# Another order of issue for a fused attention and feed-forward kernel, and its last 26 unread products left out

## The chip, the cores and the metric

The kernel runs on one core of a Trainium2 chip. The metric is the device time of one execution in microseconds, 303.65 us as the median of three runs of the kernel before. One more execution was recorded by the hardware profiler; its trace is what the views below are taken from. The engines are TensorE (PE in the views, its weight loads PEld), VectorE (DVE), ScalarE (ACT), GpSimd (POOL) and SyncE (SP), which issues nearly all DMAs. Each works through its own instructions in the order in which the program gives them, and waits on semaphores for the others.

## What is computed

Attention in which each query sees only the keys that share its nearest centroid, then a feed-forward block with SiLU:

```
q, k, v: (4, 8, 768, 64)   centroids: (8, 16, 64)   w_in: (512, 2048)   w_out: (2048, 512)
q_assign = argmax(q_n . c_n);  k_assign = argmax(k_n . c_n)
mask = q_assign[:, :, :, None] == k_assign[:, :, None, :]
scores = where(mask, (q k^T) / sqrt(64), -1e9);  attn = softmax(scores);  x = attn v
h = x @ w_in;  out = (h * sigmoid(h)) @ w_out          # x as (3072, 512), out (3072, 512) float32
```

## The kernel before

`build` (line 174) makes a graph of 1,913 steps: it says what each step does, on which engines it may run, after which steps, and with which buffers. It gives no order. The order stands in `PLAN` (line 20), a compressed list of numbers worked out beforehand by a search over a model of the engines. The list has two parts: for each of 1,307 uses of a buffer, which of the pool's buffers it gets (`POOLS`, line 138: for instance 8 banks `M` of PSUM, 20 tiles `P`, 4 tiles `hl`); then pairs of a step's number and the choice among its engines. The kernel function (line 823) unpacks the list and issues the steps one after the other (line 861). A negative number stands for products of zeros on TensorE that nothing reads. So the list alone decides which engine does what, in which order each engine works, and which buffers have to come free. The costs in the graph (`act_w`, `dve_w`, `pool_w`, lines 158 to 169) belong to the search; the kernel does not use them when it runs. In them a VectorE instruction costs 62 ns and about 1.04 ns for each element, whatever went before it.

The steps that the text speaks of, with their lines:

- Loads (L224, L243, L274, L279): k and q rows (`nat`), v rows (`nv`), the weights in 16 pieces through `gq`. All but one are issued by SyncE.
- Preparing a head (`part`, line 373). `hi` rounds the rows to float16 (L413 on ScalarE, L415 on VectorE, L417 on GpSimd) and `lo` makes the remainder (L421, VectorE). Both are turned around: by products with an identity on TensorE (L447), settled by a copy (L463 ScalarE, L465 VectorE), or by a DMA transpose that SyncE issues (L474) and that waits for `lo`. Then come the products with the centroids (L488, L493), sums and peaks (L502, L540, L545), a one-hot mark (L507, L549), its turn (L447 or VectorE's L562), and the writing of the marks under the turned rows: L525 and L527 in the one form, four writes a part on GpSimd (L574), ScalarE (L576) or VectorE (L578) in the other.
- `attention` (line 593): score products (L619), the exponential on ScalarE (L625), products with v (L642), the reciprocal and the scaling on VectorE (L658, L661), a turn to the layout of the next stage (L679 by DMA; L689 on TensorE with L696 on VectorE).
- `mlp` (line 705): products with w_in (L721), tanh on ScalarE (L727), the gate on VectorE (L730), products with w_out (L747), a copy out of PSUM (L760 ScalarE, L762 VectorE) and the store (L765). Casts of the weights stand at L293 (GpSimd) and L297 (VectorE), those of v at L254 (GpSimd) and L256 (ScalarE).

Batch 0 has its queries in two rounds (columns 0 to 1, then 2 to 5), so that feed-forward products are to be had early; the other three batches have one round. The list weaves attention of one batch with the feed-forward of the batch before, so that TensorE has something to do while ScalarE takes the exponentials. Some products of zeros (L865) stand at the start, where TensorE has nothing else. Behind the list, lines 873 to 879 issue 26 more products of zeros (L877) into four banks; nothing reads them.

Of the kernel before, what the change touches and what calls it, by code (L numbers as in the profile page):

```python
# [17 lines left out]


PLAN = (  # L20
    "c-mFk1-uqT8^+;%`*hOX-5^MZ(%mH`CEbl8DT+u*qY{F2gMxs9AWA6UM+r)!f=Y;hQs4ico%5>lyLcuxW~X+~LC0|%kK=XR|2+KhnOwl}lMXr|"
# [4 lines left out]
    "%egV8ML{zIlFe8LO`jy#bR_i=X3m5-H)QS@YwzujPQ2+^kEx5ceU@lO-fe?p#@EA@f+ihf`_MgC;}kS~;jT_SZ?w6mJD=S)d(BuTnszv*-*mkQ"
    "^Tht}z7Vvdl`?*QJHy?)-;R^l^qJcS{(r4OPk2p+%&{Ib6CE=Tg5jeQ%-FkYGSbY#fVqdyjHRD8rCd4M%(bBD<v6=zBvY=nl4PF7ZB4+e-hgdi"
    "l1XVr`Ak2k=i+Vae5Oxz)hOG_l=&G)j3vgHdk4&HP=6%ad;3hw0%q>Vo9hSdeiCC=zdOH^%{mL2D<zoc^PAPDzKgVTRlSmEuI@GWNwT|Og6T{3"
    "ZL-;2^!$FiXL`&%-TQlKPtcA}gzfP_cz^STcR!Drd%l0|`aZj^+%@e!lh=-K%3kV(S7E?j#~Y3w`zO)vPeD8L6HG6J%%2FjD@*^ym|k*MdaT`j"
    "eYWrPgvsIddh9zSXlAI-j&sQDQ2}$^lzHcv8SnOGw7G_R#VFG=p74IF^Wx1tJ*F<&)M(uY?QY<;JB81@1AJyA<IKAxV0ZbD8IwpeXEd9F;ob<@"  # L30
    "nV(>v*KbSRwUdk}GY{PNiRNOQnN3=Cj(Hl#zVW>Ft>_Jx`NONseUtj_%JPTDz#Cq7{&25&Z5x6n25hf-?Hk<ppYiqD9nLY)Z})>>c;)-;xcI`e"
    "%WL2H?w;n@`QWzGXUqNex;{I{LiYK5;WEeG(P!@NGpoaE`_vO|XTa_?e%tnxz6jap_u7&3hi7Xb+)npv=AStpwC4o=^<Ci)-_H~Ny72wy9>MT;"
    "lGpATA=~qQD`<DTkbQ1{_zdSi*LR=E^PkoQ>@Jit^Mm2@QpU?;cPYm{z1Qwj-f%zr?QZXu1Z*$6JGsxU0k3`HpuMKgj$O#MEojFuWXIDNeh-K2"
    "4(tm*jpJkw&jfdtK6{qR9JdgQ%vyKMuBvrboil0>pFRsYwd_8nFO8bEmlDi-*>PT>tPZg@@$oaiQ<roP^h7VTLwj^UJ=8}7G(tzaYd1t=(!Gg&"
    "&=;wZ2A%LNj^QZ!AqT!eTJ*<2<TSg#<1|52G(&T|hxhR^I-@JPV*vO2nfMDn!Uwp4oA?#K;V_P13szz)(jfyDqYJv3=MFfRNMFDe^Zs(2C0L3N"
    "sZUQ_#sIV+UdHdZiWSr?$1-H6J|}XcC3UUr+wmf9;Wl2yYiNU)I41|kW<+c9d5CQ(%j9wQu3Y#GtB{$pEXaja<hS7(uHz?Ur92yo;yIMY=ad&G"
    "-XWgCU7XhQP_~-525YenZ(uSCQn#MCiFRzn8PX*v`ycTvPNF3FF~q{eyeNe2<d35m>5qwfaRT|s=f@|cOA)^(p2H68#CdGS1{9&bJ{q7Q8etIS"
    "gHeF=>%_6xjh5tFp*h|pUxxTRYT^K@qby#)IO@N{1Pnn7%4%T`>2kyw#7R8siy8~k`-wA&vrw6I6;wnejHhfO$5tiX80Ap`P4Fpo`|t(c!W8V%"
    "e5Y<du?F#N;vnJ(3`0}3m$EO_HjN9`pc<xXZ4lof4%K=fJruQ32h%ifDgOb(Fp{#u#4MOj-EiV?%2r|(>SC~c`GnxnxL^k&GzZl#s(-{N4ys3f"
    "B<azl*OGpsd8;|9@%Hd8C&nNWQFxd7*_flXNq!*y)LPY=AU@C@Li)b;4dPeYdo*9LQ*%l4T<bz}hByxkxc5`-bC`?y<j+z+3ZwBgWq;tF))x8K"  # L40
    "&<^d<N$Wv-2C<;lH1Q!Zlh!@yL;Bt$_Q1=Un>eU7LOg?W@WKZ_vQn3d_!seS?T@6pq8qMbHXdm`X$>J3aR_KVBZv)%M=$i&+{IYUL8L|>9M)Rq"
    "Iva_7k%%;S14T5ih;Jc}`h%Dj6Oj&cut{?s3y>ZeH1D)#wT3jeHCM3<yRj7u^&Grdwh$+2o?`;?(MQ*abFm!T)b|{>S$$31L;OsANP04Hk)Dfm"
    "Pkhb<>qVTUu_C^TshZE2r}?5ejOpl3T>;GpVjuKHXLLbV6z7Fk0wqxj?`iBcuB6{5et^X&L;g98;hfh|m~;{Br7iu)=Oukedj)YHaS4{<2#%sZ"
    "#|%Je>WgX5AUzS2P)P47;vfu0K90$c5Y~`ii!xgOtc~+r>j&+P)cr`jfQz`QeVOC-VjtFF1!Y5sLop0Rb#H7^KWj{|9vkp0*M5i_JkL$e`%UwQ"
    "@^KiCN}N{@%hjL66~s#%bD4AMlmCePU*xZF{z}r7DO*L{if!14?f6@BS^Et2b+KDxjasB@V>Rh2#OJk-ll~OnaQwG=|4>$1-zU^Zqbfe8{u6wL"
    "7s*%0?;Lwf^N_OR8VBMDy=!RON%aZG48<wZ%c%Ph-)UX3C~Ht&6J_xM<%_WdA89`$_M^N%(sS$p;y}$Ey@T{l)H@B2Id(qBeyM$&d|AB@IIcW~"
    "VK^!vBW`ibZM~aFH$*kOfHrs)ui*~$ckzezJ<Q_T6)A74Ympv-_M|&tB<V)P7HEma=!Wj-h)!sNrf7x-^vOMR=R<H1`N3#~7{nnSeb5D6(Hed6"
    "HTOA$!+42&J3OInPqpWf?u;*}+mC1Nho^HDN5~(=0o<p23T1EOOY$D|3x|#%9wa}K_?6Z+u8^LtxqulsNSkMB4N+cB`?>l=-(Te4Ast|RrYen0"
    "n5OgLquft?1wHT<$G(ecT8reT5Z~7P)psoU03XR;aWAjtJbGfK<~9<Mgk+?`o4Ou)p*OzeI&Tms<7fPWwOEHy7>ye^rsK4pw5O53to6qJn1-9C"
    "!(`1r$}?-u)2=GirKbE%wO#W?-|@6FJuj4>v>#LUI>urg?(@v!i8t{p7HOZuQY^z2^(k>C9^x;}3#7#-*nz*XkmK@jpDd)aVm9VzpVV5>+@&3>"  # L50
    "iP?}H$2mSX$M@hR_o4O<?TuKhYtz=*TC+UMcJe1k=g@wqv0*MoQ=frzmypj%`xjCF9xuH8<PYFG(m(6{L3$qMBe&)pc3~^FX@9^1wH?199oL*d"
    "%!ND}BlSNbDZk1+PHO+qy2NcnQ68bSN<2mUAII$0v*Dc9ChpO`6U6fxW35%jW<BXW*nmg4#(AfSXK<4ADO@9c7>~7f@Ko!L`#jS;<@w9`yiOtV"
    "g>hE<2Qe1cwcn9%jvD0uP=9D`={eM9Y}7uF&1y6Lq)j{RkB<eo_EFN`;564dgYQWXp{^Ht<5Tj3h=Y*{nel_(ImkjfE1pL-<luU9xW-()Ysi1D"
    "_aX|CE&?wukiUpa@Q@#eNq7xo@CM3a00!b5*UCj4kM~JeAjTmcIk{f~F%d~fP5vF?Gz`OVe5pM|`-k=_OrUHc-o{k?q&-o6srg3igT6S=z1|{D"
    "(Y!@J^hAF>KXo;U*}2~a;vuaw;#ef3D7H|RhWcWpi=zZCQx+taL|r^b{YGMGVm;y}Y{m$T)L84AhxjI@V+K-T0jje$J|yNMmLZnHa`g%Mg~T5@"
    "_X6gSo{JUu2zfCN6;TP>upO0A1xqmsqt)N|09Ek<ZLEf6r03%z*Y3u>UL`#fv+yo<U?*PW*ppf-Xsdqa_@D87kmp8el)+-HZ9Jy#2^NulPji{{"
    "Jv`NWMQg$RXBuZ6>H27ZU-Yh^thLrA8lnx_p%LZlHOJX=wh*^!{!!+GANgo|eqsR>#JAKR!(aL~(f0=F8)`4dl|^HYX@U^tE3r!BM)@w{O^$nn"
    "vef^oy^Qh}q^oPpbshYvZyRDATtOL*nS^q}vA3zegS)89i|K34E3~Ap6>6%@<X2;j?x}qW$8iGJv<^5XNzcPIYY~6rTIGqq6Z2EHR^x_Cx-R)!"
    "l-H)d5&6bwqIsh=ibB-aW(=E>j^>ycL?9AT=t})Oy|0MvHSa0=S!06xls`bM#)kTbx<BO=$d|y!q(4C`>H_40>Q~fetU6HM5xcPmowVMmi$_WH"
    "rf<q~UPaQmiJxho!FSk;efUCakoscyAL#^Q8;)&@%%m%!GD@KenxcZPiBzOhV>oST#<^)o*Py(Pkgkh9qz`Cs(HbIM8TBZCftZDu74=Bh$4J`y"  # L60
    "E5{ww_k-3Fb=7pN#z*6Th1~0?_E5@3an4KV$$9OFz0|)Lf$Y@hz&Bdw#9WxqxwWW!nX(SV=DaHolRkoGx)=3b8OP?DN5sAylbiH;>hlm!YpjW9"
    "wBMjJ=U*pw(ffvD(^B`n(!}B@g1l%!SvQW2<(Oprq;XRJp$LlNvGz*chjd<~<Gg-EFMN2Su~yq@<7na(o;f427&4(a5|M<G)TQVA45-TSQ^}{M"
    "{CCX};v!_EE<N!@;yKFGlFooCD8cb*h?BKvVF5nJ-yHV{-!n&VX;0?bw~4d0*J}*9)@#HucpU@KMe~&Mjz~woI&lv%9yLghB~C;G(hczr>Akq4"
    "wvvBa^A-b93i~xjbvzpC`x}k)?SmNYJ?=jbI9)k+JooNQdJFDxo`>kyI>H2uLpP3lkN7_FY2PB=)m~0)#`!I@4s>7qsr9ON4CPtK52K$J6PI8J"
    "mf`{R2Q*GxYb)^^e2ZnAbA)&lS@9LV)_T`Is&@<NAeLi0o@yV*P}1GG)+^|NY2>Hl4?PpsVLh^GK68)k#1JCzNbfz$W)NqhkiLnDD=-TmYu+Ie"
# [757 lines left out]
def kernel(  # L823
# [49 lines left out]
    free = sorted(last, key=last.get)[:4]
    for rows, count in ((128, 3), (64, 6), (128, 2), (32, 8), (64, 2), (32, 4), (128, 1)):
        for i in range(count):
            r0 = i * rows % 128
            e.nc.tensor.matmul(  # L877
                e.T["M"][free[i % 4]][:, 0:256], e.zeros[r0 : r0 + rows, 0:128], e.zeros[r0 : r0 + rows, :], start=True, stop=True
            )


# [28 lines left out]
```

## Time and profile before

| | |
|---|---|
| median of three runs (lowest, highest) | 303.65 us (303.47, 304.11) |
| the profiled execution's own time | 304.88 us |
| its span, first to last instruction | 303.1 us |
| mean granted TensorE clock in it | 1.000 |
| DMA read and written | 27.30 MB and 6.29 MB |

The profiled execution took 304.88 us, of which 303.1 us are the span that the views show and 1.78 us lie around it; it was 1.23 us above the median. Busy times of TensorE include a modelled end of each product, so idle time that the views give for it is a lower bound.

### The profile page before, as it was taken

The numbers are of one execution on the slowest core, as the hardware profiler recorded it, in microseconds if no ns is written. First come the engines' busy times: TensorE is split into PE (matmuls) and PEld (weight loads), VectorE is DVE, ScalarE is ACT, GpSimd is POOL, SyncE is SP. The second block draws the span as 40 slices with busy tenths as digits, with TensorE's granted clock in tenths as the row PEclk, the third lists the DMA queues.
The fourth block names the chain that finished last, engine by engine and source line by source line (L and its number), as shares of the span: only waits on it lengthen the run. The fifth ranks groups of instructions, "written<-read, shape, count | busy, mean of one in ns | idle before, by whom it ended". The sixth has DMA issues, their size and how long they took to land.

```text
span 303.1 us, 7937 instructions
## 1 busy us (share of the span) xinstructions
PE 295.3 (97%) x3080; PEld 184.4 (61%) x3080; DVE 210.9 (70%) x519; ACT 232.1 (77%) x478; POOL 76.2 (25%) x144
## 2 busy tenths in 40 slices
PE   8888999999999999999999999999999999999998
PEld 5656776646565566666665656566666555565445
DVE  4899999999897697789999997446742312377310
ACT  3799999989989798999967888899896650468101
POOL 2534556263630436243303333000000000000000
DMA  6999999999699999998978955111000521400022
GB/s 200 313 236 163 199 263 288 251 287 247 194 241 234 274 206 263 253 297 194 266 208 149 239 89 115 26 71 28 0 3 0 64 61 28 160 15 0 35 97 79
DMA packets 80182, 48.00 MB, mean 158 GB/s; under 512 B 57360, under 2 KB 75152, under 8 KB 80144
## 3 DMA queue, kind: packets, MB, share of 16 engines
q1 hardware_dynamic: 79856, 47.39, 66.9%
q8 instruction: 24, 0.39, 0.6%
q10 hardware_dynamic: 288, 0.10, 0.1%
q14 instruction: 14, 0.11, 0.1%
HBM read 27.30 MB, written 6.29 MB: 111 GB/s over the span
## 4 chain that ended last, share of the span: by engine, by line
PE 79%; DVE 9%; DMA 6%; issue 2%; ACT 1%; SPq 1%; POOL 1%; POOLq 0%; DVEq 0%; ACTq 0%
PE M L747 27%; PE M L721 24%; PE M L619 16%; PE M L642 9%; DMA nv<-in_v_dram 2%; DVE hl L421 2%; PE M L493 2%; DMA gq<-in_moe_w_in_dram 2%; DMA nat<-in_k_dram 2%; DVE ab L578 1%; DVE gq L730 1%; ACT P L625 1%; DVE ab L527 1%; DVE M L540 1%; PE M L877 1%
## 5 line engine op out<-in xcount | busy, mean ns | idle before, releaser
L625 ACT ACTIVATE P<-M 128x512 f16<-128x512 f32 x288 | 154.8, 621 | 17.0 <-PE M L619 16.2
L721 PE MATMUL M<-xt,win_s 128*128 128x384 f16 (+2 forms) x512 | 94.3, 325 | 0.6 <-DVE gq L730 0.4
L747 PE MATMUL M<-wout_s,gq 128*128 128x512 f16 (+1 forms) x400 | 91.4, 370 | 0.0
L730 DVE SCALAR_TENSOR_TENSOR gq<-tn,M 128x384 f16<-128x384 f32 (+2 forms) x128 | 65.9, 548 | 35.0 <-ACT tn L727 34.0
L619 PE MATMUL M<-ab 80*128 80x256 f16 (+1 forms) x384 | 87.7, 326 | 2.1 <-DVE ab L527 1.0
L727 ACT ACTIVATE tn<-M 128x384 f32<-128x384 f32 (+2 forms) x128 | 60.6, 513 | 15.8 <-PE M L721 12.1
L721 PEld LDWEIGHTS <-win_s 128*128 128x128 f16 x512 | 49.1, 97 | 34.6 <-issue 0.7
L747 PEld LDWEIGHTS <-gq 128*128 128x128 f16 x400 | 38.5, 97 | 37.8
L642 PEld LDWEIGHTS <-P 128*128 128x128 f16 x1152 | 42.5, 97 | 8.4 <-issue 1.2
L619 PEld LDWEIGHTS <-ab 80*128 80x128 f16 x384 | 33.3, 97 | 20.4 <-DVE ab L527 1.9
L642 PE MATMUL M<-vt,P 128*128 128x65 f16 x1152 | 45.1, 193 | 0.4 <-DVE oh L549 0.4
L574 POOL TENSOR_SCALAR ab<-ohT 16x384 f16<-16x384 f16 (+1 forms) x54 | 29.2, 544 | 62.1 <-PE M L619 19.6
L421 DVE SCALAR_TENSOR_TENSOR hl<-nat,hl 128x384 f16<-128x384 f32 (+1 forms) x60 | 36.6, 626 | 0.6 <-ACT hl L413 0.4
L760 ACT COPY ot<-M 128x512 f32<-128x512 f32 (+1 forms) x16 | 9.0, 560 | 26.8 <-PE M L747 21.1
L417 POOL TENSOR_SCALAR hl<-nat 128x384 f16<-128x384 f32 (+1 forms) x35 | 19.2, 559 | 22.9 <-DMA nat<-in_k_dram 8.5
L540 DVE TENSOR_REDUCE M<-M 128x192 f32<-128x384 f32 (+1 forms) x28 | 15.1, 541 | 6.9 <-PE M L493 6.6
L661 DVE TENSOR_TENSOR xn<-M,rz 128x384 f16<-128x384 f32 (+2 forms) x40 | 18.7, 472 | 0.9
L762 DVE COPY ot<-M 128x512 f32<-128x512 f32 x9 | 6.0, 683 | 18.7 <-PE M L747 18.7
L254 POOL CAST vt<-nv 128x384 f16<-128x384 f32 x25 | 14.4, 589 | 15.4 <-DMA nv<-in_v_dram 14.9
L562 DVE STREAM_TRANSPOSE ohT<-oh 128x384 f16<-128x384 f16 (+1 forms) x28 | 15.5, 555 | 0.8
L578 DVE TENSOR_SCALAR ab<-ohT 16x384 f16<-16x384 f16 (+1 forms) x43 | 14.6, 342 | 1.2
L493 PEld LDWEIGHTS <-ab 128*128 128x128 f16 x320 | 11.7, 96 | 6.2 <-issue 1.5
(51 smaller groups left out, 145.3 us busy)
## 6 DMA issues: line engine op xcount, KB each, us to landing
nv<-in_v_dram SPq DMA_DIRECT2D x16, 384.0 KB, 5.2
out_dram<-ot SPq DMA_DIRECT2D x23, 256.0 KB, 2.5
nat<-in_k_dram SPq DMA_DIRECT2D x15, 384.0 KB, 5.2
nat<-in_q_dram SPq DMA_DIRECT2D x12, 384.0 KB, 4.6
gq<-in_moe_w_in_dram SPq DMA_DIRECT2D x8, 512.0 KB, 6.4
gq<-in_moe_w_out_dram SPq DMA_DIRECT2D x8, 512.0 KB, 5.6
nat<-in_q_dram SPq DMA_DIRECT2D x4, 256.0 KB, 5.5
ab<-hl SPq DMA_TRANSPOSE x32, 4.7
```

The lines of the kernel that those rows point to most:

```text
L417: e.nc.gpsimd.tensor_scalar(out=dh, in0=src, scalar1=sign[kind], scalar2=1.0, op0=ALU.mult, op1=ALU.mult)
L421: e.nc.vector.scalar_tensor_tensor(out=dl, in0=src, scalar=sign[kind], in1=dh, op0=ALU.mult, op1=ALU.subtract)
L540: e.nc.vector.tensor_reduce(out=sums(), in_=bank(Lb)[:, 0 : 32 * n].rearrange("p (n c s) -> p n c s", s=2, c=HC), axis=AX.X, op=ALU.add)
L574: e.nc.gpsimd.tensor_scalar(out=dst, in0=src, scalar1=OHV, scalar2=1.0, op0=ALU.mult, op1=ALU.mult)
L619: e.nc.tensor.matmul(bank(sb)[:, at : at + 128 * (c - a)], ab[0:80, kt[m], :], ab[0:80, qt[a] : qt[a] + c - a, :].rearrange("p n c -> p (n ...
L625: e.nc.scalar.activation(out=T(P)[:, 0:n], in_=bank(sb)[:, 0:n], func=AF.Exp, bias=0.0, scale=-ESC if negated(b, h) else ESC)
L642: e.nc.tensor.matmul(bank(O)[:, (D + 1) * t : (D + 1) * t + D + 1], T(P)[:, at : at + 128], T(vb)[:, VW * m : VW * m + D + 1], start=(m == ...
L661: e.nc.vector.tensor_tensor(out=T(xn)[:, 0:nq, (h % 2) * D : (h % 2) * D + D], in0=o3()[:, :, 0:D], in1=T(rz)[:, 0:nq].unsqueeze(2).to_bro ...
L721: e.nc.tensor.matmul(bank(bk)[:, 0:n], e.win_s[:, r, ts(fb, 128)], T(X)[:, r, 128 * j0 : 128 * j1], start=(r == 0), stop=(r == NR - 1),)
L727: e.nc.scalar.activation(out=T(tn)[:, 0:n], in_=bank(bk)[:, 0:n], func=AF.Tanh, bias=0.0, scale=1.0)
L730: e.nc.vector.scalar_tensor_tensor(out=gq(fb // 4)[:, fb % 4, 0:n], in0=T(tn)[:, 0:n], scalar=1.0, in1=bank(bk)[:, 0:n], op0=ALU.add, op1= ...
L747: e.nc.tensor.matmul(bank(bk)[:, 0 : c1 - c0], gq(quarter)[:, fc % 4, ts(t, 128)], e.wout_s[:, fc, c0:c1], start=(fc == 0), stop=(fc == NF ...
```

## The change

Two things are changed: the text of `PLAN`, and the products behind the list.

```diff
 PLAN = (
-    "c-mFk1-uqT8^+;%`*hOX-5^MZ(%mH`CEbl8DT+u*qY{F2gMxs9AWA6UM+r)!f=Y;hQs4ico%5>lyLcuxW~X+~LC0|%kK=XR|2+KhnOwl}lMXr|"
...
+    "c-l>x2i#B9AII;#zxC{C?-dedWMyRUjBMF^@7+KW*|Q?0tO$h?)juQ3C=w!4A(cuplPLf9=iKxBJTI^J^ZB0dIrrRi&-tG3xxf43IF92wo)fTt"
...
 )
@@ -857,7 +858,6 @@
-    last = {}
     for at in range(0, len(order), 2):
@@ -866,17 +866,6 @@
             s.fn(list(s.engines)[choice])
-            for b in s.use:
-                if b.pool == "M":
-                    last[b.i] = at
-
-    free = sorted(last, key=last.get)[:4]
-    for rows, count in ((128, 3), (64, 6), (128, 2), (32, 8), (64, 2), (32, 4), (128, 1)):
-        for i in range(count):
-            r0 = i * rows % 128
-            e.nc.tensor.matmul(
-                e.T["M"][free[i % 4]][:, 0:256], e.zeros[r0 : r0 + rows, 0:128], e.zeros[r0 : r0 + rows, :], start=True, stop=True
-            )
```

The graph, the costs in `build` and the pools stay as they are. The model with which the new list was searched took VectorE to need extra time between two steps of different kinds; that model is not part of the kernel. Unpacked, the two lists hold the same 1,913 steps. 1,048 of the 1,307 buffer numbers differ, and these steps change their engine:

| steps | before | after |
|---|---|---|
| writes of the marks, VectorE / ScalarE / GpSimd | 56 / 18 / 54 | 44 / 18 / 66 |
| `hi`, VectorE / ScalarE / GpSimd | 10 / 15 / 35 | 12 / 8 / 40 |
| casts of the weights, VectorE / ScalarE / GpSimd | 4 / 0 / 12 | 1 / 1 / 14 |
| casts of v, ScalarE / GpSimd | 7 / 25 | 5 / 27 |
| copies after a turn (L463, L465), VectorE / ScalarE | 2 / 3 | 1 / 4 |
| copies of the output, VectorE / ScalarE | 9 / 16 | 17 / 8 |
| products of zeros at the start, in their groups | 20, 7, 4, 5 | 20, 7, 4, 1, 4 |

Everything else keeps its engine, but not its place. Two marks serve to compare the orders, since TensorE has done the same work at them in both lists. Mark A is the first score product of batch 1: 143 steps of TensorE stand ahead of it in both lists, the same ones but for four. Mark B is the first score product of head 2 of batch 1, with 192 steps ahead of it in both. An engine's list up to the last of its steps that TensorE's steps ahead of the mark depend on has this many steps:

| | VectorE | ScalarE | GpSimd |
|---|---|---|---|
| up to mark A, before / after | 118 / 107 | 79 / 78 | 38 / 47 |
| up to mark B, before / after | 154 / 136 | 110 / 107 | 53 / 64 |

By kind, VectorE's list up to mark A has seven writes of marks of 16x256 (L578) fewer, and one each fewer of: cast of a weight (L297), copy of 128x1024 after a turn (L465), `hi` of 128x384 (L415), sum (L540), peak (L545), copy of 128x512 (L696); and one more write of marks of 16x256 in the other form (L527) and one more `hi`, of 128x512 (L415). ScalarE's up to mark A has one exponential (L625), one `hi` of 128x512 (L413) and one write of 16x256 (L525) fewer, one copy of 128x1024 after a turn (L463) and one write of 16x256 (L576) more. GpSimd's has eight writes (L574) and a cast of a weight more. VectorE's up to mark B has seven writes (L578), the weight's cast (L297), the copy (L465), three `hi` of 128x384 (L415), three `lo` of 128x384 (L421), three gates of 128x512 and two of 128x256 (L730) fewer, and the same two more.

ScalarE's list begins with `hi`, two small copies of the centroids, `hi`, a copy of 128x512 (L463) and one of 128x1024, a write (L525) and two exponentials before; after, with `hi`, the two small copies, a copy of 128x512, one of 128x1024, two writes (L525), two more copies of 128x1024, and then the exponentials. SyncE's list has the same loads and transposes; the first five loads are the same, then loads of v and of q change places, and the pieces of w_in come in the order 1, 4, 5, 0, 2, 3 in place of 4, 0, 1, 2, 5, 3, with the same transposes between them. The last four products with w_out, the copy of their 128x256 by ScalarE and its store end both lists.

More of the change, by code (lines that the diff above doesn't have):

```diff
@@ L26 @@
[L26 to L65, printed above, removed]
@@ new lines @@
+    "9aDCkkP}41PQ>_vlvVFgQaNmJO$+~e*Z4!m>zN*0u9Y1$cGz4Qq3oG<zIwK`$|2iF#1O;|T90Gz?U?(!=3mBGJ=3de?ie&ZyXG!_-$5r0PbyYC"
+    ">X>@9Q|}>jSI68f5z-lBis?BFsd!?d<5RnMG?gpU?Oj7ok|_n8IPmYLKGV=-@XYwtCWanksYyV?X1p1*6g1a(=2?@?ll#5-&#fN9kYwA(;7c&0"
+    "Q(eT&sK?knGw-pGX4k~U8)C!}(<;H<KVVi%bC7KB9X6hb=^@3`g|QON>getfM&odQ*UXM<yqe!sGv5J56fsw%L}$st7i*r}$rMW&^XQrpJNEhf"
+    "bqv|Io^9=#xy@K_C%W3MohvWub))wTa!-$^3fpLK%)0BjGzST0T_Uz^x}CqE8F$dkK&puWf2BOzyZQ)oZP45$-b7c}tVh7MOgGnhcK)?W$=E5B"
+    "v=)if#o5S?n5%;}hC-$X^{bWfd(t(I8G~z{)H6N0riT>Mf6%V3Yf2e=C_TFKTyytCdk5VqEjmN4d9H}LYn-tn=6*3IDix)kjRijj{MZWF>%B}X"
@@ L76 @@
+    "_eb;<oi}>#(|0*oO1ZP%5wJVy9SB<M+YLOb-@96Co!{6sv@Y0hz(t*Rl<VnRmwt~jmfUC?=mK4#0W{P%EA1=Ve-CA`yXkwTawNP7%eb~2zV7-B"
+    "teAx}a2Ee^bOo%0Rg_n24kC;nDnJ=13*{gJF%S!X)9x1hqxGV^23-qp>Aj79)}!YjJ9RnWs@}EWy59XLSAnV!go;oJDnkgu5C`#)0L`E|w16h?"
+    "7&L|3I-|5FwceCFLMO-xxga;xfSPcFHh<||UF$@-CDejeP!H-u1Nf8r%i6o}pYnnK-=3V>PzUNlLudqz!37TjPz|cXqmTlrkOu9bJ#>K1&;=49"
+    "36dcX<b{0D8rnb~=nMUzEp&zcFd)LYj%I<Za7pimXi+Ez#bF=}g8QKa<c9(<7=}PWC<KLJC=`JQpd^%n2jL+o4a2x!H?%wSfZ@;+dg1Slj)0Lc"
+    "3P!^i7z_Ug)Mn7m"
 )
```

59 lines of the change are left out of this document (45 added, 14 removed).

## The prediction

> **What bounds the kernel now.** I read the page's busy line first, then the table of busy time by stretch, then TensorE's waits in the early part.
>
> ```profile
> span 303.1 us, 7937 instructions
> PE 295.3 (97%) x3080; PEld 184.4 (61%) x3080; DVE 210.9 (70%) x519; ACT 232.1 (77%) x478; POOL 76.2 (25%) x144
> ```
>
> TensorE is busy for 97% of the span. A new order can win only where TensorE idles, so the question is where that is. The table by stretch has, after the stretch and its length, the busy time of TensorE, its weight loads, VectorE, ScalarE and GpSimd with their instructions, then granted clock, DMA share and GB/s:
>
> ```profile
> core 0: us, PE busy (x) PEld busy (x) DVE busy (x) ACT busy (x) POOL busy (x), PEclk, DMA share, GB/s
> 7.15:25.00 17.85, 15.29 (x238) 11.46 (x239) 15.87 (x42) 14.86 (x28) 7.05 (x11) 1.00 1.16 258
> 25.00:50.00 25.00, 24.06 (x424) 18.05 (x420) 23.54 (x76) 24.30 (x50) 15.00 (x27) 1.00 1.07 239
> 50.00:76.00 26.00, 24.72 (x246) 15.59 (x246) 25.00 (x57) 24.27 (x54) 12.06 (x19) 1.00 1.09 253
> 76.00:120.00 44.00, 43.48 (x476) 26.29 (x475) 34.76 (x84) 39.02 (x81) 17.86 (x31) 1.00 1.02 236
> 120.00:251.40 131.40, 131.40 (x1380) 81.94 (x1379) 89.40 (x215) 109.04 (x227) 21.99 (x40) 1.00 0.54 121
> 251.40:299.90 48.50, 48.50 (x277) 26.64 (x274) 19.38 (x39) 17.72 (x39) 0.00 (x0) 1.00 0.18 62
> ```
>
> From 120 us to the last useful product TensorE has no idle time that this view shows, and VectorE and ScalarE have plenty. Before that it idles for 17.85 - 15.29 = 2.56 us, then 0.94, 1.28 and 0.52 us: 5.30 us in all, a lower bound, since the ends of products are modelled. From 25 to 76 us VectorE is busy for 48.54 of 51 us and ScalarE for 48.57: two full queues feed an engine that is nearly full itself. What TensorE waits for from 7 to 76 us (total, times, longest), the first three rows:
>
> ```profile
> engine line waited for: us in total, times, longest us
> PE M L619 <- DVE ab L527: 1.0, 2, 0.8
> PE M L493 <- DVE gq L730: 0.7, 1, 0.7
> PE M L447 <- DVE hl L421: 0.5, 2, 0.3
> ```
>
> VectorE is the one that ends these waits. So the early part is a race of VectorE's and ScalarE's lists against TensorE's, and after 120 us the work of TensorE alone counts, which the change does not touch.
>
> **The change part by part.** First mark A, the first score product of batch 1. TensorE does the same work ahead of it in both lists, and the trace has it here, in the timeline:
>
> ```profile
> 52.91 0.60 PE L619 MATMUL M<-ab 80*128 80x256 f16 x3
> ```
>
> VectorE's list up to there loses and gains the kinds that the section on the change names. Their rows from the groups by shape, the last figure before the idle time being the mean of one in ns; the last three serve for mark B:
>
> ```profile
> L578 DVE TENSOR_SCALAR ab<-ohT 16x256 f16<-16x256 f16 x7 | 1.8, 259 | 0.2
> L297 DVE CAST win_s<-gq 128x1024 f16<-128x1024 f32 x1 | 0.8, 820 | 0.0
> L465 DVE COPY ab<-M 128x1024 f16<-128x1024 f16 x1 | 0.7, 690 | 0.2 <-PE M L447 0.2
> L415 DVE TENSOR_SCALAR hl<-nat 128x384 f16<-128x384 f32 x10 | 4.7, 475 | 0.1
> L540 DVE TENSOR_REDUCE M<-M 128x192 f32<-128x384 f32 x24 | 13.5, 560 | 6.9 <-PE M L493 6.6
> L545 DVE TENSOR_REDUCE mx<-M 128x12 f32<-128x192 f32 x24 | 8.5, 353 | 0.6
> L696 DVE COPY xt<-M 128x512 f16<-128x512 f16 x4 | 1.7, 419 | 0.0
> L527 DVE TENSOR_SCALAR ab<-M 16x256 f16<-16x256 f16 x6 | 1.7, 289 | 0.2
> L421 DVE SCALAR_TENSOR_TENSOR hl<-nat,hl 128x384 f16<-128x384 f32 x48 | 27.9, 596 | 0.2
> L730 DVE SCALAR_TENSOR_TENSOR gq<-tn,M 128x512 f16<-128x512 f32 x16 | 10.5, 678 | 0.2
> L730 DVE SCALAR_TENSOR_TENSOR gq<-tn,M 128x256 f16<-128x256 f32 x16 | 6.1, 414 | 0.4 <-ACT tn L727 0.3
> ```
>
> Off VectorE go 7 x 0.259 = 1.81, 0.82, 0.69, 0.475, 0.56, 0.353 and 0.419, together 5.13 us. On it come 0.289 and one rounding of 128x512, by my estimate 0.475 x 512/384 = 0.63. So VectorE can be at mark A 4.2 us sooner. ScalarE can not. Its rows:
>
> ```profile
> L463 ACT COPY ab<-M 128x1024 f16<-128x1024 f16 x2 | 2.0, 1012 | 1.0 <-PE M L447 1.0
> L625 ACT ACTIVATE P<-M 128x512 f16<-128x512 f32 x288 | 154.8, 621 | 17.0 <-PE M L619 16.2
> L413 ACT ACTIVATE hl<-nat 128x512 f16<-128x512 f32 x2 | 1.3, 630 | 4.7 <-DMA nat<-in_k_dram 4.7
> L525 ACT ACTIVATE ab<-M 16x256 f16<-16x256 f16 x2 | 0.7, 374 | 0.0
> ```
>
> It gains a copy of 1.01 us and a write priced like L525's, 0.37, and loses 0.62, 0.63 and 0.37: -0.24 us, the same work as near as I can say. With VectorE 4.2 us ahead, ScalarE becomes the later of the two, and what it can win is its own idle time. That is 0.70 us from 25 to 50 us (25.00 - 24.30), about what TensorE idles there (0.94). Term 1 is therefore 0.7 us. Its bounds: a gain of 1.6 if some of the 2.56 us before 25 us goes too, and a loss of 2.1 if the exponentials start late (rival (b)).
>
> Mark B, the first score product of head 2, is this row, with equal work ahead of it again:
>
> ```profile
> 74.83 1.03 PE L619 MATMUL M<-ab 80*128 80x256 f16 x8
> ```
>
> VectorE's list up to it is 18 steps shorter. Seven writes, the cast and the copy are 3.32 us as above, three roundings 1.43, three remainders 3 x 0.596 = 1.79, and the gates 3 x 0.678 + 2 x 0.414 = 2.86; less the 0.92 that is added, that is 8.5 us. VectorE has 1.00 us of idle time in the whole stretch from 50 to 76, and one of the waits above is a wait for gates, of which five fewer stand ahead now. With this much less in front, VectorE should cease to be late, and most of TensorE's 1.28 us should go. Term 2 is 0.8 us: 1.28 less what is left for new small waits. Its bounds are 0 and 1.3. From 76 to 120 us there are 0.52 us to win; I take 0.2 (bounds -0.3 and 0.5), because the waits there are short and a new order makes new ones. From 120 us on the term is 0: nothing idles, and the eight output copies that move to VectorE are hidden there, where it is busy for 89.40 of 131.40 and 19.38 of 48.50 us. Uncovered, one of them would cost the 0.1 us by which VectorE is slower at it; the last copy of all stays on ScalarE. A new order can also lose up to 0.3 us there.
>
> What GpSimd takes over costs it little. It is busy for 15.00 of 25 and 12.06 of 26 us; nine more steps up to mark A are, at 0.52 us, 4.7 us and fit, as long as nobody waits for a write that now takes longer:
>
> ```profile
> L574 POOL TENSOR_SCALAR ab<-ohT 16x256 f16<-16x256 f16 x9 | 4.7, 520 | 4.8 <-PE M L642 3.5 <-DVE xn L661 0.8
> ...
> L578 DVE TENSOR_SCALAR ab<-ohT x43: 218/252/995, 18.1 to 203.2; 16x384 f16<-16x384 f16 x36, 16x256 f16<-16x256 f16 x7
> ```
>
> The second of them, the view of one line, has minimum, median and maximum: a write of one of two near sizes takes VectorE 252 ns as a rule and up to 995, so something slows it down by up to four times. [...]
>
> The 26 products at the end. The chain of waits ends with them, but the store ends no sooner (its line's view, first and last start, then landing times):
>
> ```profile
> 299.94 2.07 PE M L877 x26
> L765 SPq DMA_DIRECT2D out_dram<-ot x25: 332/338/1553, 112.2 to 300.4; - x25
> DMA to landing us min/median/max: 1.7/2.5/5.6
> ```
>
> They end at 302.01 us; the last store is issued at 300.4 and lands at the soonest 1.7 us later, at 302.1. Leaving them out is worth 0 to 0.1 us at most, and I take 0.
>
> The sum is 0.7 + 0.8 + 0.2 + 0 + 0 = 1.7 us. The profiled execution would go from 304.88 to 303.2 us, its span from 303.1 to 301.4; taken off the median of 303.65 it makes 302.0 us.
>
> **The rivals.** (a) The collisions of VectorE and GpSimd eat the gain. Up to mark A GpSimd has nine steps more; if each held VectorE up for its whole 0.52 us, that is 4.7 us, more than the 4.2 us saved, VectorE stays last, and the time stays at 303.6. For it speaks the 995 ns above; against it, that the median of that row is 252, close to the minimum, and that seven of the writes that can be held up have left VectorE. [...]
>
> (b) ScalarE starts late, and the kernel gets slower. Before, this run of exponentials is the start of its full load:
>
> ```profile
> 15.65 3.72 ACT L625 ACTIVATE P<-M 128x512 f16<-128x512 f32 x7
> ```
>
> The new list puts two copies of 128x1024 more ahead of the first exponential, each of which waits for a load, its rounding and a turn on TensorE. Up to the full run one of them is new work, 1.01 us, and a rounding of 0.63 has left, so by work alone the run starts 0.4 us later. If one of these copies waits for its data, everything behind it on ScalarE waits, and ScalarE has no slack to make it up: 0.70 us from 25 to 50. A start after 15.65 + 1.7 = 17.4 us eats all that I forecast; at 18.5 us, 2.85 late, the time is 303.65 + 2.85 - 1.7 = 304.8.
>
> (c) The transfers end last, and nothing changes. The DMA share is at 1.07 and 1.09 in these stretches, and both lists move the same bytes in nearly the same order; then products that wait for a piece of w_in or a transposed head come no sooner. Only term 3 and a little of the others are left, and the time is 303.4. Against it: none of the three longest waits of TensorE above names a DMA.
>
> **How the numbers follow.** The forecast has a chance of 0.68, with its own range from 300.6 (a gain of 3.05, nine tenths of the better ends 1.6 + 1.3 + 0.5, which will hardly all be met) to 303.0. Rival (a) has 0.08, (c) 0.08 and (b) 0.16. A difference of 0.2%, 0.6 us, is about what a measurement of this kernel tells from none. So faster has 0.68, same 0.16 and slower 0.16. The range for 8 in 10 runs from 300.6 to 304.4: about 0.08 lies below it, and half of (b) above.
>
> **What would show it.** Right: TensorE's idle time falls to about 0.3 us from 25 to 50 and below 0.6 from 50 to 76, VectorE's share there falls under 0.95, ScalarE is named in most waits that are left, and the stretch after 120 us still has no idle time; the last useful product ends near 298.3 us. Wrong: the full run of exponentials starts after 17.4 us; the writes L578 and remainders L421 take longer on the mean than 0.25 to 0.36 and 0.6 us; or new gaps stand behind 120 us.

## The result and the profile after

| | before | after |
|---|---|---|
| median beside each other (lowest, highest; four runs each) | 303.56 us (303.27, 304.11) | 300.56 us (299.89, 300.92) |
| ratio, 95% interval | | 0.9897 [0.9874, 0.9919] |
| the profiled execution's own time, its span | 304.88, 303.1 us | 300.69, 298.9 us |

The change makes the kernel faster by 3.0 us, 1.0%; 1.7 us had been forecast, and the median lies just below the 300.6 to 304.4 us in which it was expected. The two profiled executions differ by 4.2 us, more than the medians, because the one of before lies 1.2 us above its median.

The busy line of the page after, to be held against that of before:

```profile
span 298.9 us, 7864 instructions
PE 292.6 (98%) x3054; PEld 184.1 (62%) x3054; DVE 212.2 (71%) x513; ACT 227.0 (76%) x463; POOL 86.9 (29%) x165
```

The table by stretch after, with the columns as before (TensorE, its weight loads, VectorE, ScalarE, GpSimd, then clock, DMA share, GB/s):

```profile
7.15:25.00 17.85, 16.12 (x260) 12.25 (x261) 16.20 (x43) 15.54 (x29) 10.91 (x19) 1.00 1.18 261
25.00:50.00 25.00, 24.99 (x434) 19.50 (x434) 22.78 (x72) 25.00 (x53) 16.01 (x27) 1.00 1.04 248
50.00:76.00 26.00, 26.00 (x263) 16.12 (x261) 23.82 (x55) 25.07 (x55) 15.57 (x25) 1.00 0.95 262
76.00:120.00 44.00, 43.83 (x488) 26.76 (x487) 38.22 (x90) 38.65 (x76) 17.05 (x29) 1.00 1.02 250
```

TensorE's idle time went from 2.56 to 1.73, from 0.94 to 0.01, from 1.28 to 0.00 and from 0.52 to 0.17 us: 5.30 us became 1.91. What the table shows besides is who the partner of TensorE is now. ScalarE is busy for all of 25 to 50 us, and VectorE has 2.2 us to spare in each of the two stretches in the middle, where it had 1.46 and 1.00. TensorE's waits from 7 to 76 us after, the first three rows:

```profile
PE M L448 <- DVE hl L422: 0.6, 3, 0.2
PE M L448 <- DVE hl L508: 0.3, 1, 0.3
PE M L489 <- ACT ab L464: 0.2, 1, 0.2
```

(In the kernel after, each line from `build` on has a number higher by one.) The waits for the marks L527 and for the gates L730 are gone. What is left lies ahead of 25 us.

Where the time was won can be read only from steps that have equal work ahead of them, and not every step has. The score products of head 2 of batch 0 come much sooner after than before. In the timeline of before (start, length, what; in brackets the idle time ahead and what ended it), first VectorE's rows and then TensorE's:

```profile
14.82 1.70 DVE L421 SCALAR_TENSOR_TENSOR hl<-nat,hl 128x512 f16<-128x512 f32 x2
16.44 0.28 DVE L545 TENSOR_REDUCE mx<-M 128x8 f32<-128x128 f32 x1
16.75 0.56 DVE L527 TENSOR_SCALAR ab<-M 16x768 f16<-16x768 f16 x1
...
17.37 0.83 PE L619 MATMUL M<-ab 80*128 80x256 f16 x6 [0.83 <-DVE ab L527]
```

And in the timeline of after, VectorE's rows, the same products on TensorE, and ScalarE's exponentials:

```profile
13.51 0.65 DVE L422 SCALAR_TENSOR_TENSOR hl<-nat,hl 128x512 f16<-128x512 f32 x1
14.25 0.76 DVE L528 TENSOR_SCALAR ab<-M 16x768 f16<-16x768 f16 x2
...
15.06 0.83 PE L620 MATMUL M<-ab 80*128 80x256 f16 x6
...
15.46 32.94 ACT L626 ACTIVATE P<-M 128x512 f16<-128x512 f32 x67
```

Before, VectorE did two remainders (1.70 us) and a peak ahead of the write that TensorE stood waiting for; the products began at 17.37 us. After, that write has one remainder ahead of it, the products begin at 15.06, and the wait of 0.83 us is gone. But these products do not have equal work ahead of them. Unpacked, the list of before has the three score products of head 3 and their three exponentials ahead of them, and the list of after has these behind them. The count of exponentials that ScalarE has begun is a fairer clock: the 7th begins at 17.80 us before and at 17.39 after, the 25th at 26.76 and 26.06, and the 73rd, the first behind mark A, at 53.39 and 51.01. So 0.70 us is won up to the 25th, and 1.68 us from there to the 73rd, in which ScalarE does the same 48 exponentials and five tanh in both kernels. The table's rows for that stretch, before and after (their counts take in instructions that reach over the ends):

```profile
26.76:53.39 26.63, 25.46 (x426) 19.14 (x425) 25.11 (x77) 25.74 (x55) 16.62 (x29) 1.00 1.13 239
```

```profile
26.06:51.01 24.95, 24.94 (x428) 19.59 (x427) 22.62 (x71) 24.95 (x54) 16.49 (x28) 1.00 1.04 253
```

ScalarE's idle time went from 0.89 us to nothing, and its busy time for the same instructions fell by 0.79 us as well. In three more traces of the order of after this stretch takes 24.94 us each. The difference lies in how ScalarE is fed. After, it takes 67 exponentials without a gap, the row above; before, they came in runs of 7, then of 19, 16 and 16:

```profile
19.55 9.41 ACT L625 ACTIVATE P<-M 128x512 f16<-128x512 f32 x19 [0.18 <-PE M L619]
29.17 7.95 ACT L625 ACTIVATE P<-M 128x512 f16<-128x512 f32 x16 [0.20 <-PE M L619]
37.31 8.27 ACT L625 ACTIVATE P<-M 128x512 f16<-128x512 f32 x16 [0.19 <-PE M L619]
```

That a gap costs more than its idle time fits with this: exponentials that follow each other without a gap overlap, as the figures of the last section show.

### The profile page after: what moved, and what is told of

It reads as the page before. It is cut to its first block, busy times and chain, and to the rows that moved or that the text cites. A ratio compares the mean times of both kernels' runs of the same rounds, so it can differ in the third digit from the quotient of the medians.

```text
span 298.9 us, 7864 instructions
## 1 busy us (share of the span) xinstructions
PE 292.6 (98%) x3054; PEld 184.1 (62%) x3054; DVE 212.2 (71%) x513; ACT 227.0 (76%) x463; POOL 86.9 (29%) x165
## 4 chain that ended last, share of the span: by engine, by line
PE 90%; DVE 3%; ACT 3%; DMA 2%; issue 1%; SPq 1%; POOL 0%; DVEq 0%; ACTq 0%; POOLq 0%
PE M L748 27%; PE M L722 27%; PE M L620 19%; PE M L643 11%; PE M L494 2%; ACT P L626 2%; DMA nat<-in_k_dram 2%; DVE hl L422 1%; PE M L448 1%; PE M L489 1%; SPq L225 1%; PE M L690 0%; DVE M L541 0%; DVE gq L731 0%; DVE oh L550 0%
## 5 line engine op out<-in xcount | busy, mean ns | idle before, releaser
L731 DVE SCALAR_TENSOR_TENSOR gq<-tn,M 128x384 f16<-128x384 f32 (+2 forms) x128 | 67.4, 549 | 23.3 <-ACT tn L728 21.2
L728 ACT ACTIVATE tn<-M 128x384 f32<-128x384 f32 (+2 forms) x128 | 62.4, 517 | 26.1 <-PE M L722 25.1
L575 POOL TENSOR_SCALAR ab<-ohT 16x384 f16<-16x384 f16 (+1 forms) x66 | 33.8, 514 | 55.5 <-DVE ohT L563 21.3
L422 DVE SCALAR_TENSOR_TENSOR hl<-nat,hl 128x384 f16<-128x384 f32 (+1 forms) x60 | 39.5, 674 | 0.6 <-ACT hl L414 0.2
L763 DVE COPY ot<-M 128x512 f32<-128x512 f32 (+1 forms) x17 | 11.4, 670 | 39.6 <-PE M L748 39.5
L418 POOL TENSOR_SCALAR hl<-nat 128x384 f16<-128x384 f32 (+1 forms) x40 | 22.1, 564 | 17.0 <-DMA nat<-in_q_dram 5.9
L255 POOL CAST vt<-nv 128x384 f16<-128x384 f32 x27 | 15.6, 587 | 12.6 <-DMA nv<-in_v_dram 11.9
L761 ACT COPY ot<-M 128x512 f32<-128x512 f32 (+1 forms) x8 | 4.5, 562 | 15.1 <-PE M L748 15.1
L494 PE MATMUL M<-stk,ab 128*128 128x32 f16 x320 | 12.3, 176 | 0.0
```

What stands on the lines that cost most here:

```text
L418: e.nc.gpsimd.tensor_scalar(out=dh, in0=src, scalar1=sign[kind], scalar2=1.0, op0=ALU.mult, op1=ALU.mult)
L422: e.nc.vector.scalar_tensor_tensor(out=dl, in0=src, scalar=sign[kind], in1=dh, op0=ALU.mult, op1=ALU.subtract)
L494: e.nc.tensor.matmul(bank(Lb)[:, 32 * i : 32 * i + 32], w, e.stk[:, sg, hh].rearrange("p c s -> p (c s)"), start=True, stop=True)
L575: e.nc.gpsimd.tensor_scalar(out=dst, in0=src, scalar1=OHV, scalar2=1.0, op0=ALU.mult, op1=ALU.mult)
L728: e.nc.scalar.activation(out=T(tn)[:, 0:n], in_=bank(bk)[:, 0:n], func=AF.Tanh, bias=0.0, scale=1.0)
L731: e.nc.vector.scalar_tensor_tensor(out=gq(fb // 4)[:, fb % 4, 0:n], in0=T(tn)[:, 0:n], scalar=1.0, in1=bank(bk)[:, 0:n], op0=ALU.add, op1= ...
```

## The experiments

Three groups of four. Each group ran on one chip beside the kernel before, which had 303.05 us there in the first, 303.94 in the second and 303.82 in the third. One and the same kernel starts up differently from one execution to the next: the kernel after reached the same step at 15.95 us in one trace and at 16.82 in another. The second and third groups are therefore also compared by a stretch that begins behind this: from the first exponential of head 2 of batch 0 (called P from here on) to the first exponential of batch 1, just behind mark A. In the traces P to A takes 35.59 us before (17.80 to 53.39) and 35.06 us after (15.95 to 51.01). Six exponentials stand ahead of P in the order of before and three in that of after, so P and P to A serve only to compare kernels of one order.

### First group: the parts of the change by themselves

**The products at the end put back into the kernel after.**

```diff
+    free = sorted(last, key=last.get)[:4]
+    for rows, count in ((128, 3), (64, 6), (128, 2), (32, 8), (64, 2), (32, 4), (128, 1)):
+        ...
```

> The kernel after, with the 26 unread products issued behind the list again. Theory (the whole gain is the list's): no change against the kernel after, 300.6 us, ratio to before 0.990, since the last store lands no sooner than the products end. Rival (the products held the end up): up to 0.3 us slower than after, 300.9 us.

Measured: 300.65 us, ratio to before 0.9918 [0.9891, 0.9945], beside 0.9897 [0.9874, 0.9919] without them. The difference is within the intervals; the span is 298.5 us against 298.9. The products cost nothing that can be measured, and the list makes the gain.

**The order and buffers of before, with each step on the engine that it has after** (127 steps move; without the products at the end). As an edit of the unpacked list:

```diff
-order = before
+order = [(step, engine_after[step]) for step, engine in before]
```

> The old list in its order and with its buffers, but each step on the engine that the new list gives it (127 steps differ); no products at the end. VectorE's list up to mark A is then 107 steps (118 before, 107 after), up to mark B 141 (154, 136). Theory 1 (the steps taken off VectorE make the gain): two thirds of the gain or more, 301.6 us or less. Theory 2 (the order makes the gain, the engines only fit it): under a third of it, 302.7 us or more, perhaps slower than before.

**The order and buffers of after, with each step on the engine that it had before.**

```diff
-order = after
+order = [(step, engine_before[step]) for step, engine in after]
```

> The new list in its order and with its buffers, but each step on the engine that the old list gives it. VectorE's list up to mark A is 115 steps (118 before, 107 after), up to mark B 149 (154, 136). Theory 1 (VectorE's load): most of the gain is lost, 302.4 us or more. Theory 2 (the order): most is kept, 301.5 us or less.

Measured: 328.9 us, ratio 1.0857 [1.082, 1.0895], for the first, and 323.62 us, ratio 1.0672 [1.0625, 1.0718], for the second. Neither half does any good alone; each by itself costs 21 to 26 us. In the first, with VectorE's list up to mark A as short as after (107 steps), TensorE waits from 7 to 120 us as follows (first three rows; the line numbers in this kernel and in the next one are lower by one than before):

```profile
PE M L641 <- ACT vt L255: 3.0, 1, 3.0
PE M L446 <- DVE hl L420: 2.7, 4, 2.0
PE M L487 <- ACT ab L462: 1.7, 2, 1.5
```

The cast had moved from GpSimd to ScalarE, and the copy of the longest wait in the third row from VectorE to ScalarE. In a queue at a place meant for another engine they came 3.0 and 1.5 us too late for TensorE, and what stands behind such a step can come late as well. So "VectorE's lists are shorter" cannot be a sufficient reason, though term 1 of the forecast rests on it: the choice of engine and the place in the list are one decision.

**The list of after up to mark A, then the rest in the order of before.** Buffers as in the one and the other where they are free.

```diff
-order = after
+order = after[:A] + [step for step in before if step not in after[:A]]
```

> The new list up to the first score product of batch 1 (mark A), then the steps that are left in the old list's order, on its engines and in its buffers. Theory 1: the part up to A gives what TensorE's idle time before 50 us lost, some 1.7 us, and the wait for VectorE in the old part stays at least in part: 301.3 to 302.2 us. Theory that the early part alone sets it all: 300.6 us. Theory that the part behind A gives most: 302.5 us or more.

Measured: 310.86 us, ratio 1.0258 [1.0226, 1.029]. Up to 50 us it does what after does; then the seam shows. Its table by stretch and TensorE's waits from 50 to 76 us:

```profile
25.00:50.00 25.00, 24.99 (x434) 19.51 (x431) 22.76 (x73) 25.00 (x53) 16.18 (x28) 1.00 1.17 262
50.00:76.00 26.00, 19.57 (x135) 10.02 (x133) 17.96 (x39) 16.67 (x36) 8.10 (x12) 0.87 0.71 200
76.00:120.00 44.00, 44.00 (x483) 27.27 (x482) 35.57 (x86) 40.05 (x82) 18.64 (x32) 1.00 0.95 238
```

```profile
PE M L720 <- DVE gq L729: 3.0, 1, 3.0
PE M L618 <- DVE gq L729: 2.5, 1, 2.5
PE M L641 <- DVE gq L729: 0.9, 1, 0.9
```

The loss of some 10 us against after is nearly all in one stretch: 6.43 us of idle TensorE, and a mean clock of 0.87 over its 26 us, at most 26 x 0.13 = 3.4 us more. It comes from joining two lists and says nothing of how the gain is split at mark A. This run did not answer its question.

### Second group: who has slack

Since lists cannot be mixed, the theory was tested with small added work. It says: before, VectorE's list set the early part, with ScalarE's close behind; after, ScalarE's does, and VectorE has some 2 us to spare. The rival: a list that was searched for its own times suffers from any delay alike. Four instructions of 128x384 that nothing reads are put on one engine, behind TensorE's steps 60, 80, 100 and 120; in the traces they run between 27.9 and 47.0 us. (A setting of their source, 0.38 us on VectorE at 1.1 us, comes with them.)

```diff
         s.fn(list(s.engines)[choice])
+        if list(s.engines)[choice] == "PE":
+            pe += 1
+            if pe in (60, 80, 100, 120):
+                e.nc.vector.tensor_scalar(out=e.j16, in0=e.j32, scalar1=2.0, scalar2=None, op0=ALU.mult)
```

and for ScalarE, in place of the last line,

```diff
+                e.nc.scalar.activation(out=e.j16, in_=e.j32, func=AF.Copy, bias=0.0, scale=2.0)
```

Before, with VectorE's:

> The kernel before with four roundings of 128x384 on VectorE added that nothing reads (4 x 0.475 = 1.9 us), behind TensorE's steps no. 60, 80, 100 and 120, that is between about 25 and 50 us. Theory (before, VectorE's list set the early part and ScalarE's was close behind; afterwards ScalarE's and TensorE's own work set it and VectorE has about 2 us to spare in each of the stretches from 25 to 50 and from 50 to 76 us): nearly all of it is paid, +1.4 to +2.0 us against before. Rival (any delay in an early list costs alike, whichever engine has it, since the order only fits its own times): the same figure in all four kernels of this group, +1 to +2 us each. Second rival (the gain is not one of an engine's load but of another order of transfers): below +0.5 us.

Before, with ScalarE's:

> The kernel before with four copies of 128x384 on ScalarE added that nothing reads (about 4 x 0.48 = 1.9 us), at the same places. Theory: ScalarE had 0.70 us idle from 25 to 50 us and 1.73 from 50 to 76 before, so a part of it is covered: +0.6 to +1.6 us against before. Rival (any delay costs alike): as much as the kernel with VectorE's four roundings, within 0.4 us. Second rival (transfers): below +0.5 us.

After, with VectorE's:

> The kernel after with the same four roundings on VectorE (1.9 us). Theory: VectorE's idle time of 2.2 us from 25 to 50 us takes them, 0 to +0.5 us against after. Rival (any delay costs alike): +1 to +2 us against after, as for the kernel before.

After, with ScalarE's:

> The kernel after with the same four copies on ScalarE (1.9 us). Theory: ScalarE is busy for 25.00 of 25 us and 25.07 of 26 there, so it is now the list without slack: +1.2 to +2.0 us against after. Rival (any delay costs alike): as much as VectorE's four roundings cost after, within 0.4 us. If TensorE alone sets the time now and ScalarE's queue only looks full: below +0.5 us.

| | median | ratio to before | P to A | longer by |
|---|---|---|---|---|
| before + VectorE | 305.68 us | 1.0070 [1.0038, 1.0102] | 37.34 us | 1.75 us |
| before + ScalarE | 303.88 us | 1.0006 [0.9984, 1.0029] | 36.09 us | 0.50 us |
| after + VectorE | 301.83 us | 0.9938 [0.9916, 0.9960] | 35.46 us | 0.40 us |
| after + ScalarE | 302.83 us | 0.9967 [0.9946, 0.9988] | 36.80 us | 1.74 us |

The stretch P to A answers plainly: the two engines have changed places. VectorE's instructions, 350 to 764 ns each, cost 1.75 us before and 0.40 after; ScalarE's, 523 to 844 ns, cost 0.50 before and 1.74 after. The rival would have wanted one figure four times, and the second rival less than 0.5 us for VectorE's before. One figure lies outside what the theory expected: ScalarE's cost before was put at 0.6 to 1.6 us and is 0.50, so more of it was covered. The row from 25 to 50 us of each kernel's table by stretch, in the same sequence, shows it as TensorE's idle time:

```profile
25.00:50.00 25.00, 22.45 (x384) 16.20 (x381) 23.95 (x74) 22.40 (x45) 13.12 (x24) 1.00 1.07 257
```

```profile
25.00:50.00 25.00, 24.03 (x418) 17.79 (x416) 22.87 (x75) 25.00 (x53) 14.32 (x27) 1.00 1.09 234
```

```profile
25.00:50.00 25.00, 24.67 (x431) 18.85 (x429) 23.60 (x75) 24.75 (x52) 16.28 (x28) 1.00 1.07 254
```

```profile
25.00:50.00 25.00, 24.16 (x402) 17.86 (x401) 21.48 (x67) 24.98 (x53) 14.82 (x27) 1.00 1.05 245
```

In the first, the 1.87 us that were added to VectorE leave TensorE idle for 2.55 us (0.94 without them), and ScalarE is starved too, with 22.40 us. In the second, ScalarE simply fills the 0.70 us that it had, and TensorE's idle time is 0.97, as without. The medians agree for before (+1.7 and 0.0 us). For after they can only be set against its ratio in the result above and in the third group, 0.990 and 0.989: ScalarE's cost 0.7 to 0.8%, some 2.2 us, a little above the 1.2 to 2.0 expected, and VectorE's 0.4 to 0.5%, some 1.3 us, more than the 0.40 us that the trace shows and than the 0.5 us expected. Its profiled execution (300.65 us, span 298.9) shows no such loss; the intervals reach from nothing to some 3 us, so this one figure stays open.

### Third group: can the start be made better still?

If ScalarE's list sets the time after, then work taken off it ahead of its long run should pay. Two candidates stand there: a write of marks (0.41 us at 15.02 us) and a copy of 128x1024 (1.02 us at 12.99 us). The order is left alone; only the choice of engine in the list changes.

```diff
-(164, ACT)   # write of marks, L577
+(164, POOL)
-(85, ACT)    # copy after a turn, L464
+(85, DVE)
```

The kernel after as it is:

> The kernel after, unchanged, beside the three edits of it in this group and on the same chip. Every theory: the ratio to before that it had, 0.990 within 0.3%, so 2 to 4 us below before.

The write alone:

> The kernel after with one write of marks of 16x256 (at 15.02 us on ScalarE, 0.41 us, ahead of the unbroken run of exponentials) given to GpSimd; the order of issue is kept. Theory (ScalarE's list up to mark A sets the time): the run of exponentials starts about 0.4 us sooner and the time falls by 0.2 to 0.4 us. Rival (VectorE and TensorE set the start of the run, or the products with that write wait for GpSimd's slower 0.5 us): within 0.1 us, or 0.1 to 0.3 longer.

The copy alone:

> The kernel after with one copy of 128x1024 (at 12.99 us on ScalarE, 1.02 us) given to VectorE, where such a copy took 0.69 us; order kept. Theory (ScalarE sets the time, VectorE has 1.65 us idle from 7.15 to 25): the exponentials start 0.5 to 1.0 us sooner and the time falls by 0.3 to 0.9 us. Rival (VectorE is still on the path before 15 us, since TensorE's longest waits there are for its remainders): the sums and marks behind the copy on VectorE come 0.7 us later and the time stays or rises by up to 0.7 us.

Both:

> Both moves, the write to GpSimd and the copy to VectorE. Theory: the two gains add up, 0.5 to 1.3 us below after. Rival: as the copy alone.

| | median | ratio to before | P at | P to A | span |
|---|---|---|---|---|---|
| after | 300.77 us | 0.9890 [0.9859, 0.9922] | 16.82 us | 35.05 us | 299.3 us |
| write to GpSimd | 303.35 us | 0.9975 [0.9947, 1.0002] | 17.32 us | 36.07 us | 301.7 us |
| copy to VectorE | 300.68 us | 0.9900 [0.9867, 0.9932] | 16.23 us | 35.05 us | 299.3 us |
| both | 304.61 us | 1.0018 [0.9996, 1.0039] | 17.64 us | 35.99 us | 301.8 us |

For the copy the theory missed and the rival's figure fits: P comes at 16.23 us, inside what the unchanged kernel does by itself (15.95 and 16.82), and the time stays. Ahead of P it is still VectorE that ends TensorE's waits, as in the rows for 7 to 76 us above, and to take a microsecond off ScalarE there wins nothing. For the write both missed by far: 0.41 us moved costs 2.6 us, all that the change had won but 0.5. Both moves together cost 1.3 us more than the write alone, which neither expectation had and which stays unexplained. No version beats the kernel after. What the write does is a chain through three queues, which the waits of GpSimd from 8 to 20 us, the timeline of VectorE and that of TensorE of this kernel tell (its line numbers are those of before; L574 is the moved write, L417 GpSimd's rounding, L421 VectorE's remainder, L527 VectorE's write of other marks):

```profile
POOL ab L574 <- PE M L619: 4.2, 1, 4.2
```

```profile
15.36 0.69 DVE L421 SCALAR_TENSOR_TENSOR hl<-nat,hl 128x512 f16<-128x512 f32 x1 [1.83 <-POOL hl L417]
16.08 0.76 DVE L527 TENSOR_SCALAR ab<-M 16x768 f16<-16x768 f16 x2
```

```profile
16.90 0.83 PE L619 MATMUL M<-ab 80*128 80x256 f16 x6 [1.82 <-DVE ab L527]
```

In GpSimd's list the write stands ahead of a cast and a rounding. It waits 4.2 us for a score product; the rounding behind it is late; VectorE's remainder waits 1.83 us for the rounding, VectorE's write comes behind that, and TensorE waits 1.82 us for it. In the kernel after, the moved write stands in ScalarE's list, where it runs at 15.02 us without a wait. Then a second cost follows. TensorE's table by short stretches in this kernel:

```profile
14.00:16.00 2.00, 1.08 (x36) 0.95 (x33) 0.64 (x1) 1.47 (x3) 1.85 (x4) 1.00 1.09 329
16.00:18.00 2.00, 1.10 (x9) 0.84 (x10) 1.87 (x8) 0.68 (x2) 1.79 (x5) 0.90 0.42 81
18.00:20.00 2.00, 2.00 (x13) 1.29 (x12) 1.04 (x3) 2.00 (x5) 0.44 (x2) 0.50 0.89 220
20.00:22.00 2.00, 2.00 (x25) 1.46 (x24) 1.60 (x5) 1.20 (x3) 1.77 (x4) 0.74 0.99 182
```

After 4 us in which TensorE was busy for 2.18, the granted clock falls to 0.50. From 16 to 22 us it loses 2 x (0.10 + 0.50 + 0.26) = 1.7 us of full clock, part of which was idle time anyway. P to A is 1.0 us longer than without the move, though all waits lie ahead of P or close to it.

## Why the prediction was right in kind and wrong in size

The sign, the stretch (all ahead of 120 us), the engine that was relieved and the one that took its place are as forecast. Point by point:

- **Term 1, 0.7 us up to mark A: too small, and outside its own upper bound of 1.6.** This is the step that failed. It said that ScalarE could win no more than its own idle time from 25 to 50 us, 0.70 us. In the profiled pair mark A comes 2.61 us sooner by TensorE's rows and the first exponential behind it 2.38 us sooner. From the 25th exponential on 1.68 us is won, and only 0.89 us of that is idle time of ScalarE. The other 0.79 us is busy time, which the forecast took as fixed: it did not ask how much less the same instructions take when none has to wait for its input. The rest is won ahead of the 25th exponential, out of the 2.56 us in which TensorE idled before 25 us; the term took it at nothing, and only its bound allowed for some. It is 0.70 us in the profiled pair, but the start varies from one execution to the next. Three traces in the order of before have the 25th exponential at 26.76, 26.00 and 26.84 us, and six in the order of after (with the added work or products behind it, or with the copy moved) at 26.06, 25.73, 26.93, 25.99, 26.23 and 26.34: means of 26.53 and 26.21, so 0.3 us, which is within that variation. The mechanism of the term held, as the second group shows: VectorE was the later of the two before and ScalarE is after. Which feature of the new list brings this about, the shorter list of VectorE or the order within it, no run separates.
- **Term 2, 0.8 us from mark A to mark B: right, 0.87 measured.** The two marks after:

```profile
50.30 0.81 PE L620 MATMUL M<-ab 80*128 80x512 f16 x4
71.78 0.60 PE L620 MATMUL M<-ab 80*128 80x256 f16 x3
```

These are 21.48 us. Before, mark B is the fifth of the eight products of the row at 74.83 us that the prediction showed, at 75.26, and the stretch from 52.91 takes 22.35 us. TensorE has no idle time left in it after.
- **Term 3, 0.2 us from 76 to 120 us: 0.35** (idle time 0.52 to 0.17), within its bounds. Behind 120 us there is no idle time to see in either trace, as forecast.
- **The products at the end at 0: right.** Their restoration changed nothing.
- The sum by parts, 0.3 + 1.7 + 0.9 + 0.35 = 3.25 us, is near the 3.0 us of the medians. The profiled pair has more, 2.61 us at mark A by TensorE's rows, 0.87 to mark B and 0.72 from there to the end of the span; before's execution lies 1.2 us above its median. Where exactly this excess lies was not settled. The last useful product ends at 295.7 us, where 298.3 was named.
- **Rival (a), collisions of VectorE and GpSimd: seen, and covered.** All remainders after:

```profile
L422 DVE SCALAR_TENSOR_TENSOR hl<-nat,hl 128x384 f16<-128x384 f32 (+1 forms) x60 | 39.5, 674 | 0.6 <-ACT hl L414 0.2
```

And the same group before:

```profile
L421 DVE SCALAR_TENSOR_TENSOR hl<-nat,hl 128x384 f16<-128x384 f32 (+1 forms) x60 | 36.6, 626 | 0.6 <-ACT hl L413 0.4
```

The mean of 60 went from 626 to 674 ns, 2.9 us in all, with GpSimd's list fuller by 12 writes and 5 roundings. VectorE still has 2.2 us idle in each of the middle stretches, and the 1.87 us added to it in the second group cost 0.40 us there. One forecast sign of trouble, remainders above 0.6 us on the mean, thus came true (those of 128x384 alone went from 596 to 645 ns), and the time fell all the same. Rival (a) reckoned with the whole 0.52 us of a write of GpSimd's for each meeting; the traces show less. In them 26 of the 60 have a GpSimd instruction beside them before and 32 after; those take 704 and 768 ns on the mean, and the others 566 in both. Of the remainders of 128x384 alone, those with one beside them take 673 ns before and 747 after, and the others 545 and 551: 0.13 to 0.20 us more on the mean. The writes L578 before show the same: the 18 with no GpSimd instruction beside them take 255 ns at most, the 25 with one 411 on the mean and up to the 995 that the prediction names.
- **Rival (b), a late start of ScalarE: did not come, but the place was right.** The first two exponentials are later (13.89 against 12.71 us), the full run is sooner (15.46 without a gap against 15.65 with gaps). The third group shows what rival (b) looks like when it does come: one write in the wrong queue, 2.6 us.
- **Rival (c), transfers: no sign of them.** DMA shares are much as before (1.18, 1.04, 0.95 and 1.02), and none of the three longest waits of TensorE names one.

Of the signs named ahead: idle time of 0.01 us (0.3 forecast) and 0.00 (below 0.6), and VectorE's share of 0.91 and 0.92 (below 0.95) came true. ScalarE is not named in most of the waits left; from 7 to 76 us VectorE still is, with 0.9 us, because what remains lies ahead of 25 us. From 25 us on there is hardly a wait left to be named.

## What to carry to other kernels

Where two queues both look full, find out which one sets the time by adding work to each: four instructions of 128x384 on VectorE (1.87 us busy) cost 1.75 us before and 0.40 after, and four on ScalarE (2.91 and 2.71 us busy, overlapping with their neighbours) 0.50 and 1.74. In an order written out for queues that work strictly in turn, count not only what an engine's list loses but what stands ahead of the one step that another engine waits for; the engine and the place belong together, and a step moved without its neighbours can cost six times its own length (0.41 us moved, 2.6 us lost). Compare two orders only at steps with the same work ahead of them: the score products of head 2 came 2.3 us sooner here, but by the count of exponentials only 0.4 us was won there. And do not take an engine's idle time for all that it can win: here the same 48 exponentials and five tanh took 1.68 us less, of which 0.89 us had been idle time.

## What the runs showed of the hardware that was not expected

The granted TensorE clock fell to 0.50 after TensorE had been busy for about half of some microseconds: 2.18 of 4.00 us with a longest pause of 1.82 us in the kernel with the moved write. In the two kernels of the first group that mix an order with the other's engines it was busy for 1.46 of 3.00 us (13 to 16) before a clock of 0.50 (16 to 19), and for 1.29 of 3.00 us (8 to 11) before a clock of 0.51 (12 to 15); their mean clocks over the profiled spans were 0.978 and 0.989. Where it was busy for 2.93 of the 4 us from 14 to 18 (before) or 3.63 (after), the clock stayed at 1.00. But the busy share alone does not tell the fall: in the third group's trace of the kernel after TensorE was busy for only 1.41 of the 3 us from 8 to 11, with a longest pause of 1.35 us, and the clock stayed at 1.00. The rows, before and in that trace:

```profile
14.00:18.00 4.00, 2.93 (x31) 2.13 (x28) 3.84 (x8) 3.84 (x8) 2.44 (x5) 1.00 1.32 297
```

```profile
8.00:11.00 3.00, 1.41 (x31) 1.28 (x31) 1.95 (x4) 0.38 (x2) 2.55 (x4) 1.00 1.21 209
```

With the fall a misplaced step cost more than its waits: up to 1.7 us of full clock from 16 to 22 us in the kernel with the moved write. The runs do not give a rule for when the clock falls.

Exponentials that follow each other without a gap took less time than their durations add up to. Of the exponentials up to mark A there are 72 in both kernels; before and after, by groups:

```profile
L625 ACT ACTIVATE P<-M 128x512 f16<-128x512 f32 x72 | 36.4, 635 | 1.5 <-PE M L619 1.3
```

```profile
L626 ACT ACTIVATE P<-M 128x512 f16<-128x512 f32 x72 | 35.8, 820 | 0.0
```

The mean of one rises from 635 to 820 ns while the time that all of them take falls from 36.4 + 1.5 to 35.8 us: with the next one queued, they overlap, for 72 times 0.820 us is more than the 35.8 us that they fill. A mean duration of one instruction is no price when the queue is full; the busy time of the group divided by its count is, 0.497 us here.
